# Attention stage: the exchange of halves per head instead of per block, and the word operations of a w_val half spread one to a step

## The chip, the cores and the metric

One core of one Trainium2 chip runs the whole program in one launch. The metric is device time in microseconds (us), the median of repeated executions; before the change three executions took 618.32, 618.34 and 618.87 us. The profile is one further execution, taken by the hardware profiler.

## The reference

The program is a chain of three blocks on a batch of 2 with 8 heads, 768 positions and a head width of 64. Only the first and the start of the second matter here.

```python
q_bits = (einsum(q, proj) > 0); k_bits = (einsum(k, proj) > 0)     # 6 bits: 64 buckets
mask   = q_bucket[:, :, :, None] == k_bucket[:, :, None, :]
scores = where(mask, scale * q @ k.T, -1e9)
attn   = softmax(scores)                                           # exp, sum, divide
x      = attn @ v                                                  # heads side by side: [2, 768, 512]
...
gate = sigmoid(causal_conv(x, conv_w)); val = x @ w_val
x    = (gate * val) @ w_out                                        # second block
...                                                                # third block: FFT mixing, norm, two-layer MLP
```

Matrix weights arrive as float64 words. The kernel turns each into a pair of float32 numbers (high and low part) by integer operations on the words, and multiplies with three matmuls (high by high, high by low, low by high).

## The kernel before

**Pairs and steps.** `attention` goes over eight pairs of heads (p = 0 to 7), each in twelve steps (i = 0 to 11, n = 12p + i; steps are counted from 0 here, as in the code, so the change's "steps 7 to 9" are i = 6, 7, 8). Step i covers 128 query rows of one head; six steps are a head. The order on each engine is written out by hand: whatever a step calls is issued in that order to the engine's queue, and each engine takes its queue strictly in order.

**One step.** PE (TensorE) transposes the probabilities of step n (`ptp`, L593), multiplies the scores of step n + 3 (`sp`, L557, one PSUM buffer), and multiplies with v (`op`, L616, half of a 256-row block per step). DVE (VectorE) clamps the scores of n + 3 out of PSUM (`sd`, L568), then takes the low part of the transposed probabilities (`ptl`, L605). ACT (ScalarE) takes their high part (`pth`, L601), then the exponential of step n + 2 (`sd`, L575), and in odd steps copies a finished block of the product out of PSUM (`xc`, L629). In steps 9 to 11 and 1 to 3 two transposes of the next pair's q and k go beside (L693), with a high part on ACT (`ht`, L698) and a low part on DVE (`lt`, L701). In steps 4 and 5 the bucket bits are projected (`bp`, L443). `qk_place` (L411 to L416, steps 3 and 9) sends those parts by DMA from SP's queue into the tiles that the scores read. `norm_spread` (L644) and `norm_beside` (L666) turn the softmax sums of the pair before into a row that is spread by DMA; `norm_mul` (L719) applies it on POOL (GpSimd).

**The exchange of halves.** A block's product has its high-part sum in 64 partitions and its low-part sum in the other 64. `pv_out` copies the block to `xc`, sends 64 partitions of it by DMA to `xs` (one buffer; L633, on SP's queue), and a step later POOL adds the two into `xm` (L634).

**The words of w_val.** `half_weights` converts a 128 by 256 half of w_val, one half per pair (`val_weights`), with six integer operations on DVE and two on ACT. The words lie in one PSUM tile `cvp`, whose left half is `a` and whose right half is `g`. In order: *magnitude* (L271, DVE, writes a), *rest* (L272, DVE, writes g), *rest_low* (L275, DVE, writes g), *rebias* (L278, ACT, reads and writes a), *sign* (L279, DVE, writes a), *exponent* (L280, DVE, reads a, writes another tile), *low* (L283, DVE, writes `wvl`), *high* (L286, ACT, reads a, writes `wvh`). They are called in five groups, at the end of steps 6 to 10 (7 to 11 in pair 0, 0 to 4 in pair 7).

Of the kernel before, what the change touches and what calls it, by code (L numbers as in the profile page):

```python
# [17 lines left out]
P = 128  # L18
# [86 lines left out]
def block_kernel(  # L105
# [156 lines left out]
    def words_split(raw, dst_h, dst_l, b, a, g):  # L262

        n = raw.shape[1]
        words = raw.bitcast(I32).rearrange("p (n two) -> p n two", two=2)
        lo, hi = words[:, :, 0], words[:, :, 1]
        a, g = a.bitcast(I32), g.bitcast(I32)
        e = ap4.tile([P, DM], I32, tag="cve", name="cv")[:, :n]

        def step0():  # L270
            nc.vector.tensor_scalar(a, hi, 0x7FFFFE00, None, op0=ALU.bitwise_and)  # L271
            nc.vector.tensor_scalar(g, hi, 0x1FF, 15, op0=ALU.bitwise_and, op1=ALU.logical_shift_left)  # L272

        def step1():
            nc.vector.scalar_tensor_tensor(g, lo, 17, g, op0=ALU.logical_shift_right, op1=ALU.bitwise_or)  # L275

        def step2():
            nc.scalar.activation(a, a, AF.Relu, scale=8.0, bias=col[:, b : b + 1])  # L278
            nc.vector.scalar_tensor_tensor(a, hi, -(2 ** 31), a, op0=ALU.bitwise_and, op1=ALU.bitwise_or)  # L279
            nc.vector.tensor_scalar(e, a, -(2 ** 23), None, op0=ALU.bitwise_and)  # L280

        def step3():
            nc.vector.scalar_tensor_tensor(dst_l, g, 2.0 ** -35, e.bitcast(F32), op0=ALU.mult, op1=ALU.mult)  # L283

        def step4():
# [16 lines left out]
    def attention(es):  # L302
# [315 lines left out]
                        start=r == 0 and x == 0, stop=r == R - 1 and x == 1,  # L618
                    )

        def pv_out(kb):
            p, j, blk = kb // 6, (kb % 6) // 3, kb % 3
            if kb % 6 == 0:
                st[p]["xm"] = ap2.tile([P, S], F32, tag="xm", name="xm")
            mr = slice(64 * j, 64 * j + 64)
            cr = slice(64 - 64 * j, 128 - 64 * j)
            xc = ap2.tile([P, QB], F32, tag="xc", name="xc")
            xs = ap2.tile([P, QB], F32, tag="xs", name="xs", bufs=1)
            nc.scalar.copy(xc, po[kb])  # L629
            if kb == 6 * NPR - 1:  # L630
                nc.scalar.copy(xs[mr, :], po[kb][cr, :])
            else:
                nc.sync.dma_start(xs[mr, :], xc[cr, :])  # L633
            add[kb] = lambda: nc.gpsimd.tensor_tensor(  # L634
                st[p]["xm"][mr, blk * QB : (blk + 1) * QB], xc[mr, :], xs[mr, :], op=ALU.add
            )

        def norm_sums(p):
            sums = st[p]["sums"]
# [2 lines left out]
        def norm_spread(p):  # L642
            rinv = st[p]["rinv"] = ap2.tile([P, 2, R], F32, tag="rinv", name="rinv")
            nc.vector.reciprocal(rinv, st[p]["sums"].rearrange("p (j r) -> p j r", j=2))  # L644
            if p < NPR - 1:
                return
            rb = st[p]["rb"] = ap1.tile([P, R, 2, D], F32, tag="rb", name="rb")
# [124 lines left out]
        def val_load(i):  # L772
            c, h = divmod(i, 2)
            wv_raw[i] = ap4.tile([P, DM // 2], I64, tag="wvr", name="wvr", bufs=2)
            nc.sync.dma_start(wv_raw[i], w_val[c * P : (c + 1) * P, h * DM // 2 : (h + 1) * DM // 2])

        def val_weights(i):
            c, h = divmod(i, 2)
            cs = slice(h * DM // 2, (h + 1) * DM // 2)
            return half_weights(wv_raw[i], wvh[:, c, cs], wvl[:, c, cs], 3)  # L780

        def out_tile(i):
            t = qk_tile((0, 2, 1)[i]).rearrange("p a s -> p (a s)")
# [16 lines left out]
        convs = [(b, c, i) for b, c in pairs[: NPR - 1] for i in range(9)]  # L800
        start()
        NT = 12 * NPR
        for n in range(NT + 2):
# [25 lines left out]
            if n + 2 < NT:  # L829
                expo(n + 2)  # L830
            if 0 <= kb < 6 * NPR and part == 1:
                pv_out(kb)
            if n == 6:
                prep_step(1, i)
            if kb - 1 in add and part == 0:
                add.pop(kb - 1)()
            elif n == NT + 1:
                add.pop(kb)()
# [42 lines left out]
            if p < NPR and at <= i < at + 5:
                if i == at:
                    wsteps = val_weights(p)
                    if p + 1 < NPR:
                        val_load(p + 1)
                wsteps[i - at]()
# [123 lines left out]
    def mixing(es):  # L1010
# [419 lines left out]
```

## Time and profile before

| | |
|---|---|
| median of three executions | 618.34 us |
| the profiled execution's own time | 618.59 us |
| its span, first to last instruction | 616.8 us |
| PE busy | 604.7 us (98%) |
| DVE busy | 444.7 us (72%) |
| ACT busy | 358.5 us (58%) |
| POOL busy | 269.3 us (44%) |
| granted TensorE clock | 0.999 of full speed |

The attention stage lies between about 10 and 250 us of the span. A line of a timeline has the start in us from the span's start, the duration, the engine, the line of the kernel, the operation, output and inputs with their shape, and in brackets how long the engine had been idle before it and what ended that. Instructions of an engine overlap a little: the next one starts about 0.08 us before the one ahead has ended on DVE and about 0.10 us on ACT, so that what one costs its engine is the distance to the next start. In a list of windows each line gives a stretch, its length, and for each engine the busy time with the number of instructions.

### The profile page before, as it was taken

The numbers are of one execution on the slowest core, as the hardware profiler recorded it, in microseconds if no ns is written. First come the engines' busy times: TensorE is split into PE (matmuls) and PEld (weight loads), VectorE is DVE, ScalarE is ACT, GpSimd is POOL, SyncE is SP. The second block draws the span as 40 slices with busy tenths as digits, with TensorE's granted clock in tenths as the row PEclk, the third lists the DMA queues.
The fourth block names the chain that finished last, engine by engine and source line by source line (L and its number), as shares of the span: only waits on it lengthen the run. The fifth ranks groups of instructions, "written<-read, shape, count | busy, mean of one in ns | idle before, by whom it ended". The sixth has DMA issues, their size and how long they took to land.

```text
span 616.8 us, 10435 instructions
## 1 busy us (share of the span) xinstructions
PE 604.7 (98%) x3711; PEld 537.4 (87%) x3711; DVE 444.7 (72%) x850; ACT 358.5 (58%) x712; POOL 269.3 (44%) x303
## 2 busy tenths in 40 slices
PE   7999999999999999999999999999999999999997
PEld 6889999999998889998898988888888888888886
DVE  5999999999999998898669788888885411111113
ACT  5998899998998887944625355555665111111121
POOL 8152588876888799892350633233221000000000
PEclk9999999999999999999999999999999999999999
DMA  6956686756666640262110243443440200000002
GB/s 139 210 142 164 145 178 160 164 152 156 157 154 178 171 124 14 73 231 70 36 35 0 70 133 118 125 136 108 134 135 1 103 0 1 2 0 1 0 1 102
DMA packets 54957, 62.02 MB, mean 101 GB/s; under 512 B 29184, under 2 KB 42664, under 8 KB 54650
## 3 DMA queue, kind: packets, MB, share of 16 engines
q1 hardware_dynamic: 54170, 57.81, 35.7%
q0 software_dynamic: 432, 3.55, 1.5%
q8 instruction: 29, 0.48, 0.3%
q14 instruction: 22, 0.18, 0.1%
q10 hardware_dynamic: 304, 0.01, 0.0%
HBM read 36.73 MB, written 3.19 MB: 65 GB/s over the span
## 4 chain that ended last, share of the span: by engine, by line
PE 78%; DVE 10%; DMA 4%; ACT 2%; issue 2%; SPq 2%; POOL 1%; DVEq 0%; ACTq 0%; POOLq 0%
PE pf L1337 20%; PE acc L1347 20%; PE sp L557 8%; PE op L616 7%; PE ptp L593 6%; PE ps L1154 5%; PE ps L222 3%; PE ps L1218 3%; DVE sd L568 2%; DVE ptl L605 2%; PE ps L1189 1%; DMA rqk<-in_k_dram 1%; PE late L222 1%; DMA xs<-xc 1%; PE bp L443 1%
## 5 line engine op out<-in xcount | busy, mean ns | idle before, releaser
L1347 PE MATMUL acc<-w,hid 128*128 128x512 f32 x576 | 137.4, 391 | 0.0
L1347 PEld LDWEIGHTS acc<-w,hid 128*128 128x128 f32 x576 | 105.5, 188 | 20.1
L1340 DVE SCALAR_TENSOR_TENSOR hid<-pf,hid 128x512 fp32r<-128x512 f32 (+1 forms) x62 | 33.4, 555 | 120.6 <-ACT hid L1339 120.6
L1337 PE MATMUL pf<-uth,w 128*128 128x512 f32 (+1 forms) x496 | 97.1, 337 | 0.1
L568 DVE TENSOR_SCALAR_CACHE_REDUCE sd<-sp 128x768 f32<-128x768 f32 x96 | 91.1, 950 | 7.7 <-PE sp L557 7.2
L1339 ACT ACTIVATE hid<-pf 128x512 fp32r<-128x512 f32 (+1 forms) x62 | 28.9, 488 | 115.2 <-PE pf L1337 115.2
L557 PE MATMUL sp<-qk 128*128 128x512 f32 (+1 forms) x384 | 91.5, 360 | 3.9 <-DVE sd L568 2.6
L605 DVE TENSOR_TENSOR ptl<-ptp,pth 128x768 fp32r<-128x768 f32 x96 | 91.4, 952 | 5.1 <-ACT pth L601 3.8
L1337 PEld LDWEIGHTS pf<-uth,w 128*128 128x128 f32 x496 | 79.0, 188 | 15.2 <-DVE hid L1340 1.3
L575 ACT ACTIVATE sd<-sd,nm 128x768 f32<-128x768 f32 x96 | 90.1, 939 | 1.5 <-DVE sd L568 1.5
L601 ACT CAST pth<-ptp 128x768 fp32r<-128x768 f32 x96 | 77.0, 802 | 17.7 <-PE ptp L693 8.9
L162 POOL TENSOR_TENSOR w<-cv 128x512 fp32r<-128x512 f32 x31 | 40.1, 1293 | 88.8 <-DVE cv L157 77.4
L593 PE MATMUL ptp<-ident,sd 128*128 128x128 f32 x576 | 78.6, 272 | 0.2 <-ACT sd L575 0.2
L616 PE MATMUL op<-pth,v 128*128 128x256 f32 x288 | 74.0, 283 | 1.0 <-ACT xc L629 1.0
L616 PE MATMUL op<-ptl,v 128*128 128x256 f32 x288 | 73.8, 286 | 0.0
L557 PEld LDWEIGHTS sp<-qk 128*128 128x128 f32 x384 | 58.2, 189 | 13.6 <-DVE sd L568 7.1
L593 PEld LDWEIGHTS ptp<-ident,sd 128*128 128x128 f32 x576 | 65.8, 140 | 1.1 <-ACT sd L575 0.5
L634 POOL TENSOR_TENSOR xm<-xc,xs 64x256 f32<-64x256 f32 x48 | 35.2, 734 | 59.2 <-DMA xs<-xc 38.6
L616 PEld LDWEIGHTS op<-pth,v 128*128 128x128 f32 x288 | 54.2, 188 | 5.9 <-ACT xc L629 2.0
L616 PEld LDWEIGHTS op<-ptl,v 128*128 128x128 f32 x288 | 54.3, 188 | 0.3
L1337 PE MATMUL pf<-utl,w 128*128 128x512 f32 (+1 forms) x248 | 53.1, 336 | 0.0
L149 ACT ACTIVATE cv<-cv,col 128x512 int32<-128x512 int32 x32 | 23.2, 725 | 41.5 <-DVE cv L146 41.5
(214 smaller groups left out, 998.0 us busy)
## 6 DMA issues: line engine op xcount, KB each, us to landing
raw<-in_moe_w_ch_dram SPq DMA_DIRECT2D x32, 512.0 KB
qk<-ht SPq DMA_DIRECT2D x60, 192.0 KB
qk<-lt SPq DMA_DIRECT2D x30, 192.0 KB
rqk<-in_q_dram SPq DMA_DIRECT2D x16, 192.0 KB
rqk<-in_k_dram SPq DMA_DIRECT2D x16, 192.0 KB
rv<-in_v_dram SPq DMA_DIRECT2D x8, 384.0 KB
out_dram<-o SPq DMA_DIRECT2D x12, 256.0 KB
xs<-xc SPq DMA_DIRECT2D x47, 64.0 KB
```

The lines of the kernel that those rows point to most:

```text
L162: nc.gpsimd.tensor_tensor(dst()[1], fold(g.bitcast(F32)), fold(e.bitcast(F32)), op=ALU.mult)
L557: nc.tensor.matmul(sp[:, cs], q2[i][:, m, qi * P : (qi + 1) * P], k2[i][:, m, cs], start=m == order[0], stop=m == order[1])
L568: nc.vector.tensor_scalar(sd[n], sp, CLAMP, None, op0=ALU.min, op1=ALU.min, accum_out=st[p]["nm"][:, n % 12 : n % 12 + 1],)
L575: nc.scalar.activation(sd[n], sd[n], AF.Exp, bias=st[p]["nm"][:, i : i + 1], scale=-1.0, accum_out=st[p]["sums"][:, i : i + 1],)
L593: nc.tensor.transpose(tp[:, r // 3, c0 : c0 + P], sd[n][:, r * P : (r + 1) * P], ident)
L601: nc.scalar.copy(p_parts(n)[0], tp)
L605: nc.vector.tensor_tensor(lo, tp, f32(ho), op=ALU.subtract)
L616: nc.tensor.matmul(po[kb], v3[:, r, c0 : c0 + P], pt[kb][x][:, r, :], start=r == 0 and x == 0, stop=r == R - 1 and x == 1,)
L634: add[kb] = lambda: nc.gpsimd.tensor_tensor(st[p]["xm"][mr, blk * QB : (blk + 1) * QB], xc[mr, :], xs[mr, :], op=ALU.add)
L1337: nc.tensor.matmul(pf, w[:, c, :], x[:, c, cs], start=n == 0, stop=n == 3 * NC - 1)
L1340: nc.vector.scalar_tensor_tensor(hl[:, cs], pf, 0.0, f32(hh)[:, cs], op0=ALU.max, op1=ALU.subtract)
L1347: nc.tensor.matmul(acc, x[:, ts_], w, start=f == 0 and n == 0, stop=f == NF - 1 and n == 2)
```

## The change

Three edits, all in `attention` and its helper for the words.

1. `pv_out`: `xc` holds a whole head (three blocks) and `xs` is gone. The DMA goes straight into the half of `xm` that the head will own, once per head after its third block (192 KB in place of three times 64 KB), and POOL adds `xc` to `xm` once per head, two steps after the DMA is issued. The last head keeps its exchange per block, because its blocks are wanted one by one.
2. The eight word operations become functions of their own. In pairs 1 to 5 they are called in six groups at steps 6, 7, 8 and at steps 0, 1, 2 of the next pair, with one DVE operation each. Pairs 0, 6 and 7, and the words of w_out, keep their five groups.
3. In pair 7 the row of sums is transposed in step 3 rather than 1, its spreading DMA is issued in step 4 rather than 2, and the product follows in step 6 rather than 5; `rb` takes the buffer of `rv`.

```diff
+WV = (0, 1, 2, 6, 7, 8)
...
+        return magnitude, rest, rest_low, rebias, sign, exponent, low, high
+
+    def in_five(steps):
+        groups = (0, 1), (2,), (3, 4, 5), (6,), (7,)
+        return [lambda x=x: run(steps[i] for i in x) for x in groups]
...
-        def pv_out(kb):
+        def pv_out(n, kb):
...
-            xc = ap2.tile([P, QB], F32, tag="xc", name="xc")
-            xs = ap2.tile([P, QB], F32, tag="xs", name="xs", bufs=1)
-            nc.scalar.copy(xc, po[kb])
+            cs = slice(blk * QB, (blk + 1) * QB)
+            nc.scalar.copy(xc[:, cs], po[kb])
             if kb == 6 * NPR - 1:
-                nc.scalar.copy(xs[mr, :], po[kb][cr, :])
+                nc.scalar.copy(xm[mr, cs], po[kb][cr, :])
+                at = n
+            elif kb >= 6 * NPR - 3:
+                nc.sync.dma_start(xm[mr, cs], xc[cr, cs])
+                at = n + 1
+            elif blk < 2:
+                return
             else:
-                nc.sync.dma_start(xs[mr, :], xc[cr, :])
+                cs = slice(0, S)
+                nc.sync.dma_start(xm[mr, :], xc[cr, :])
+                at = n + 2
+            add[at] = lambda: nc.gpsimd.tensor_tensor(xm[mr, cs], xc[mr, cs], xm[mr, cs], op=ALU.add)
...
-            if 1 <= p and i == (1 if p == NPR - 1 else 4):
+            if 1 <= p and i == (3 if p == NPR - 1 else 4):
                 return norm_beside(p - 1)
...
+            if not 1 <= i < NPR - 2:
+                return dict(enumerate(in_five(steps)))
+            return dict(zip(WV, [lambda x=x: run(steps[i] for i in x) for x in ((0,), (1,), (2, 3), (4,), (5, 7), (6,))]))
```

Where the instructions stand now is shown at three places. **First**, DVE in steps 7 to 9 of pair 1, before:

```order
L605 TENSOR_TENSOR ptl<-ptp,pth 128x6x128
L275 SCALAR_TENSOR_TENSOR cvp<-wvr,cvp 128x256
L568 TENSOR_SCALAR sd,nm<-sp 128x768
L605 TENSOR_TENSOR ptl<-ptp,pth 128x6x128
L279 SCALAR_TENSOR_TENSOR cvp<-wvr,cvp 128x256
L280 TENSOR_SCALAR cv<-cvp 128x256
L568 TENSOR_SCALAR sd,nm<-sp 128x768
L605 TENSOR_TENSOR ptl<-ptp,pth 128x6x128
L701 SCALAR_TENSOR_TENSOR lt<-ptp,col,ht 128x256
L283 SCALAR_TENSOR_TENSOR wvl<-cvp,cv 128x256
```

and now (L616 is `ptl`, L579 the clamp, L720 `lt`; L275 is now *rest* and L278 *rest_low*):

```order
L616 TENSOR_TENSOR ptl<-ptp,pth 128x6x128
L275 TENSOR_SCALAR cvp<-wvr 128x256
L579 TENSOR_SCALAR sd,nm<-sp 128x768
L616 TENSOR_TENSOR ptl<-ptp,pth 128x6x128
L278 SCALAR_TENSOR_TENSOR cvp<-wvr,cvp 128x256
L579 TENSOR_SCALAR sd,nm<-sp 128x768
L616 TENSOR_TENSOR ptl<-ptp,pth 128x6x128
L720 SCALAR_TENSOR_TENSOR lt<-ptp,col,ht 128x256
```

*rest_low* has moved from step 7 to step 8, behind that step's `ptl`; *sign*, *exponent* and *low* have left these steps. *rebias* keeps its place on ACT, behind the exponential of step 8 and ahead of the high parts of step 9:

```order
L586 ACTIVATE sd,sums<-sd,nm 128x768 [waits DVE_49]
L281 ACTIVATE cvp<-cvp,col 128x256 [waits DVE_49,Activation_49]
L612 CAST pth<-ptp 128x6x128 [waits PE_49]
L717 ACTIVATE ht<-ptp,col 128x256 [waits DMAHW5_49,DMAHW6_49,DMAHW4_49,DMAHW3_49]
L586 ACTIVATE sd,sums<-sd,nm 128x768
L642 COPY xc<-op 128x256 [waits PE_49,Pool_49]
```

**Second**, ACT and DVE in steps 1 and 2 of pair 2. ACT from the exponential of step 1 on, before and now:

```order
L575 ACTIVATE sd,sums<-sd,nm 128x768 [waits DVE_49,Activation_49]
L629 COPY xc<-op 128x256 [waits DMAHW6_49,PE_49,Pool_49]
L601 CAST pth<-ptp 128x6x128 [waits PE_49,Activation_49]
L698 ACTIVATE ht<-ptp,col 128x256
L575 ACTIVATE sd,sums<-sd,nm 128x768 [waits DVE_49]
```

```order
L586 ACTIVATE sd,sums<-sd,nm 128x768 [waits DVE_49,Activation_49]
L642 COPY xc<-op 128x256 [waits PE_49]
L293 CAST wvh<-cvp 128x256 [waits DVE_49]
L612 CAST pth<-ptp 128x6x128 [waits PE_49,Activation_49]
L717 ACTIVATE ht<-ptp,col 128x256
L586 ACTIVATE sd,sums<-sd,nm 128x768
```

DVE there now (L287 is *exponent*, L290 *low*, L663 the reciprocal of `norm_spread`):

```order
L616 TENSOR_TENSOR ptl<-ptp,pth 128x6x128
L720 SCALAR_TENSOR_TENSOR lt<-ptp,col,ht 128x256
L287 TENSOR_SCALAR cv<-cvp 128x256
L579 TENSOR_SCALAR sd,nm<-sp 128x768
L616 TENSOR_TENSOR ptl<-ptp,pth 128x6x128
L720 SCALAR_TENSOR_TENSOR lt<-ptp,col,ht 128x256
L663 RECIPROCAL rinv<-sums 128x12
L290 SCALAR_TENSOR_TENSOR wvl<-cvp,cv 128x256
```

*high* (L293) has come from step 10 of the pair before to step 1, between the block's copy and the high part of step 2; *exponent* and *low* stand behind the `lt` of steps 1 and 2.

**Third**, SP's queue from step 7 to step 9 of pair 1, before and now (`wvr` is the next half of w_val, `rs` the spread row):

```order
L775 DMA wvr<-in_moe_w_val_dram 128x256
L633 DMA xs<-xc 64x256
L680 DMA rs<-rd 64x768 x2
L633 DMA xs<-xc 64x256
L411 DMA qk<-ht 64x768
L412 DMA qk<-ht 64x768
```

```order
L794 DMA wvr<-in_moe_w_val_dram 128x256
L653 DMA xm<-xc 64x768
L699 DMA rs<-rd 64x768 x2
L422 DMA qk<-ht 64x768
L423 DMA qk<-ht 64x768
```

The exchange of step 9 that stood ahead of `qk_place` is gone, and with it the wait for `xs`, the one buffer that POOL's add gives back.

## Rows read from the trace of the kernel before

**Rows 1.** Page, part 4: the chain that ended last, by engine.

```profile
PE 78%; DVE 10%; DMA 4%; ACT 2%; issue 2%; SPq 2%; POOL 1%; DVEq 0%; ACTq 0%; POOLq 0%
```

**Rows 2.** Windows from step 6 of pairs 2, 4, 5 to the next pair's.

```profile
89.40:117.90 28.50, 28.22 (x215) 26.72 (x214) 27.27 (x52) 25.85 (x54) 23.94 (x27) 1.00 0.72 168
...
146.39:175.57 29.18, 28.67 (x215) 26.68 (x214) 27.22 (x51) 26.58 (x57) 24.57 (x28) 1.00 0.65 154
175.57:205.04 29.47, 28.63 (x215) 26.78 (x214) 27.24 (x52) 26.53 (x55) 26.62 (x32) 1.00 0.64 161
```

**Rows 3.** Timeline of PE, steps 7 and 8 of pair 2.

```profile
89.91 0.82 PE L593 MATMUL ptp<-ident,sd 128*128 128x128 f32 x6
90.48 0.94 PE L557 MATMUL sp<-qk 128*128 128x512 f32 x4
...
91.97 0.82 PE L593 MATMUL ptp<-ident,sd 128*128 128x128 f32 x6
93.07 0.96 PE L557 MATMUL sp<-qk 128*128 128x512 f32 x4 [0.28 <-DVE sd L568]
```

**Rows 4.** Timeline of DVE, steps 7 and 9 of pair 2.

```profile
92.93 0.95 DVE L605 TENSOR_TENSOR ptl<-ptp,pth 128x768 fp32r<-128x768 f32 x1
93.80 0.42 DVE L275 SCALAR_TENSOR_TENSOR cvp<-wvr,cvp 128x256 int32<-128x256 int32 x1
...
98.41 0.47 DVE L701 SCALAR_TENSOR_TENSOR lt<-ptp,col,ht 128x256 fp32r<-128x256 f32 x1
```

**Rows 5.** Timeline of ACT, steps 8 and 9 of pair 2.

```profile
94.50 0.44 ACT L278 ACTIVATE cvp<-cvp,col 128x256 int32<-128x256 int32 x1
95.71 0.80 ACT L601 CAST pth<-ptp 128x768 fp32r<-128x768 f32 x1 [0.77 <-PE ptp L693]
96.40 0.48 ACT L698 ACTIVATE ht<-ptp,col 128x256 fp32r<-128x256 f32 x1
96.77 0.94 ACT L575 ACTIVATE sd<-sd,nm 128x768 f32<-128x768 f32 x1
...
97.69 0.37 ACT L629 COPY xc<-op 128x256 f32<-128x256 f32 x1
```

**Rows 6.** Timeline of ACT, then DVE: later conversions of w_out.

```profile
243.03 0.45 ACT L278 ACTIVATE cvp<-cvp,col 128x256 int32<-128x256 int32 x1 [0.41 <-DVE cvp L275]
...
259.98 0.59 ACT L286 CAST qk<-cvp 128x512 fp32r<-128x512 f32 x1 [0.65 <-DVE cv L280]
...
258.53 0.69 DVE L279 SCALAR_TENSOR_TENSOR cvp<-wor,cvp 128x512 int32<-128x512 int32 x1
```

**Rows 7.** Timeline: ACT and DVE in step 1 of pair 5, ACT in step 1 of pair 6.

```profile
163.38 0.47 ACT L698 ACTIVATE ht<-ptp,col 128x256 fp32r<-128x256 f32 x1 [0.67 <-DMA qk<-ht]
163.88 0.96 DVE L605 TENSOR_TENSOR ptl<-ptp,pth 128x768 fp32r<-128x768 f32 x1 [0.31 <-ACT ht L698]
...
192.89 0.47 ACT L698 ACTIVATE ht<-ptp,col 128x256 fp32r<-128x256 f32 x1 [1.00 <-DMA qk<-ht]
```

**Rows 8.** Waits of SP's queue: total us, times, longest.

```profile
SPq L633 <- POOL xm L634: 25.7, 21, 2.9
```

**Rows 9.** Timeline, DVE and PE, first steps of pair 7.

```profile
218.50 0.96 DVE L568 TENSOR_SCALAR_CACHE_REDUCE sd<-sp 128x768 f32<-128x768 f32 x1 [0.23 <-PE sp L557]
...
220.53 0.28 PE L666 MATMUL ptp<-ident,rinv 128*12 128x128 f32 x1 [0.68 <-DVE rinv L644]
...
221.54 0.96 DVE L568 TENSOR_SCALAR_CACHE_REDUCE sd<-sp 128x768 f32<-128x768 f32 x1 [0.28 <-PE sp L557]
```

**Rows 10.** Timeline, DVE, ACT and PE, steps 1 to 4 of pair 3.

```profile
106.50 0.95 DVE L605 TENSOR_TENSOR ptl<-ptp,pth 128x768 fp32r<-128x768 f32 x1
...
107.26 0.80 ACT L601 CAST pth<-ptp 128x768 fp32r<-128x768 f32 x1
...
108.79 0.95 DVE L605 TENSOR_TENSOR ptl<-ptp,pth 128x768 fp32r<-128x768 f32 x1
...
111.39 0.95 PE L557 MATMUL sp<-qk 128*128 128x512 f32 x4
```

More of the change, by code (lines that the diff above doesn't have):

```diff
@@ L268, in words_split, with magnitude, rest, rest_low @@
         e = ap4.tile([P, DM], I32, tag="cve", name="cv")[:, :n]
-        def step0():
+        def magnitude():
             nc.vector.tensor_scalar(a, hi, 0x7FFFFE00, None, op0=ALU.bitwise_and)
+        def rest():
             nc.vector.tensor_scalar(g, hi, 0x1FF, 15, op0=ALU.bitwise_and, op1=ALU.logical_shift_left)
-        def step1():
+        def rest_low():
             nc.vector.scalar_tensor_tensor(g, lo, 17, g, op0=ALU.logical_shift_right, op1=ALU.bitwise_or)
-        def step2():
+        def rebias():
             nc.scalar.activation(a, a, AF.Relu, scale=8.0, bias=col[:, b : b + 1])
+        def sign():
             nc.vector.scalar_tensor_tensor(a, hi, -(2 ** 31), a, op0=ALU.bitwise_and, op1=ALU.bitwise_or)
+        def exponent():
             nc.vector.tensor_scalar(e, a, -(2 ** 23), None, op0=ALU.bitwise_and)
-        def step3():
+        def low():
             nc.vector.scalar_tensor_tensor(dst_l, g, 2.0 ** -35, e.bitcast(F32), op0=ALU.mult, op1=ALU.mult)
-        def step4():
+        def high():
             nc.scalar.copy(dst_h, a.bitcast(F32))
-        return [step0, step1, step2, step3, step4]
+        return magnitude, rest, rest_low, rebias, sign, exponent, low, high
+    def in_five(steps):
+        groups = (0, 1), (2,), (3, 4, 5), (6,), (7,)
+        return [lambda x=x: run(steps[i] for i in x) for x in groups]
     def half_weights(raw, dst_h, dst_l, b):
@@ L624, in pv_out @@
                 st[p]["xm"] = ap2.tile([P, S], F32, tag="xm", name="xm")
+            if blk == 0:
+                st[p]["xc"] = ap2.tile([P, S], F32, tag="xc", name="xc")
+            xm, xc = st[p]["xm"], st[p]["xc"]
             mr = slice(64 * j, 64 * j + 64)
             cr = slice(64 - 64 * j, 128 - 64 * j)
-            xc = ap2.tile([P, QB], F32, tag="xc", name="xc")
-            xs = ap2.tile([P, QB], F32, tag="xs", name="xs", bufs=1)
-            nc.scalar.copy(xc, po[kb])
+            cs = slice(blk * QB, (blk + 1) * QB)
+            nc.scalar.copy(xc[:, cs], po[kb])
             if kb == 6 * NPR - 1:
-                nc.scalar.copy(xs[mr, :], po[kb][cr, :])
-            else:
-                nc.sync.dma_start(xs[mr, :], xc[cr, :])
-            add[kb] = lambda: nc.gpsimd.tensor_tensor(
-                st[p]["xm"][mr, blk * QB : (blk + 1) * QB], xc[mr, :], xs[mr, :], op=ALU.add
-            )
+                nc.scalar.copy(xm[mr, cs], po[kb][cr, :])
[5 more added lines that the diff above has]
+                return
+            else:
+                cs = slice(0, S)
+                nc.sync.dma_start(xm[mr, :], xc[cr, :])
+                at = n + 2
+            add[at] = lambda: nc.gpsimd.tensor_tensor(xm[mr, cs], xc[mr, cs], xm[mr, cs], op=ALU.add)
         def norm_sums(p):
@@ L646, in norm_spread @@
                 return
-            rb = st[p]["rb"] = ap1.tile([P, R, 2, D], F32, tag="rb", name="rb")
+            rb = st[p]["rb"] = ap1.tile([P, R, 2, D], F32, tag="rv", name="rb")
             pool_copy(
@@ L779, in val_weights @@
             cs = slice(h * DM // 2, (h + 1) * DM // 2)
-            return half_weights(wv_raw[i], wvh[:, c, cs], wvl[:, c, cs], 3)
+            steps = half_weights(wv_raw[i], wvh[:, c, cs], wvl[:, c, cs], 3)
+            if not 1 <= i < NPR - 2:
+                return dict(enumerate(in_five(steps)))
+            return dict(zip(WV, [lambda x=x: run(steps[i] for i in x) for x in ((0,), (1,), (2, 3), (4,), (5, 7), (6,))]))
         def out_tile(i):
@@ L790, in out_half @@
             cs = slice(i * DM // 2, (i + 1) * DM // 2)
-            return half_weights(wo_raw[0][:, cs], wo_h[0][:, cs], wo_l[0][:, cs], 4)
+            return in_five(half_weights(wo_raw[0][:, cs], wo_h[0][:, cs], wo_l[0][:, cs], 4))
         tail = []
@@ L798, in val_early @@
             val_matmul(0, 0, c, tail[c])
+        wsteps = {}
         convs = [(b, c, i) for b, c in pairs[: NPR - 1] for i in range(9)]
@@ L831, in attention @@
             if 0 <= kb < 6 * NPR and part == 1:
[L832 to L838, printed above, removed]
+                pv_out(n, kb)
+            if n in add:
+                add.pop(n)()
             if n == 0:
                 values(0, 1)
-            if p + 1 < NPR and n != 6:
+            if p + 1 < NPR:
                 prep_step(p + 1, i)
@@ L851, in attention @@
             last = p == NPR - 1
-            if i == (2 if last else 7) and 1 <= p < NPR:
+            if i == (4 if last else 7) and 1 <= p < NPR:
                 norm_rows(p - 1)
-            if i == (5 if last else 10) and 1 <= p < NPR:
+            if i == (6 if last else 10) and 1 <= p < NPR:
                 norm_mul(p - 1)
@@ L880, in attention @@
             at = 0 if last else 7 if p == 0 else 6
[L881 to L886, printed above, removed]
+            if p < NPR and i == at:
+                wsteps = {n + x: f for x, f in val_weights(p).items()}
+                if p + 1 < NPR:
+                    val_load(p + 1)
+            if n in wsteps:
+                wsteps.pop(n)()
             for _ in range(1 if n >= NT - 16 else 5 * n // 6 - 5 * (n - 1) // 6):
@@ L1066, in chunk @@
             a, g_ = (x.tile([P, DM], F32, tag=y, name="cvp") for x, y in ((psm, "m"), (pso, "o")))
-            return words_split(wo_raw[c], wo_h[c], wo_l[c], 4, a, g_)
+            return in_five(words_split(wo_raw[c], wo_h[c], wo_l[c], 4, a, g_))
         def gated(c):
```

## Prediction

> **What bounds the kernel now.** I read the page first. The chain that ended last is PE for 78% and DVE for 10% [rows 1], so time is lost where PE waits for something, and a change beside PE pays only as far as such a wait moves. Then the windows from pair to pair: a pair of the attention stage takes 28.50 us (pairs 1 to 3 agree within 0.01), and ACT, DVE and PE are all nearly full in it, 25.85, 27.27 and 28.22 busy; two later pairs took 29.18 and 29.47 [rows 2]. The timelines show what a step is made of. PE's bare step is 2.06 us from `ptp` to `ptp`, and in step 8 the scores start at 93.07 though the transposes were through at 92.54 (0.57 after their start, as in step 7): PE waited 0.53 for the clamp [rows 3]. The clamp was late because DVE had two word operations in step 6. A word operation holds DVE 0.34, a `ptl` or clamp 0.87, an `lt` 0.39, each its duration less the overlap of 0.08 [rows 4].
>
> A Trainium skill page, Perfetto Trace Analysis, section Identifying the Most-Contended Engine, calls busy share a fair measure of headroom for the vector and scalar engines. By that ACT has 28.50 - 25.85 = 2.65 us per pair to spare, and the two waits below would vanish in it.
>
> **What the change adds: two waits of ACT for DVE.** That is the term that decides. *rebias* (ACT) changes one half of the tile `cvp`, and *rest_low* (DVE) writes the other half ahead of it in the program. The waits go by the tile: in a later conversion *rebias* was idle 0.41 until *rest_low* (L275) ended, though *magnitude* had ended long before; and *high* (L286) was idle 0.65 until *exponent* (L280), although *sign* (L279), the last to write what it reads, had ended 0.76 earlier, at 259.22 [rows 6]. Before, this cost nothing in pairs 1 to 5: *rest_low* ran in step 7 and *rebias* in step 8, *exponent* in step 8 and *high* in step 10. Now *rest_low* and *rebias* are called in one step, and so are *exponent* and *high*, and ACT's queue holds the high parts of the next step behind them.
>
> *Wait at step 8.* Let its clamp start at t. DVE then does the clamp and `ptl` (0.87 each) and *rest_low* (0.42): ended at t + 2.16. With 0.06 for the signal, *rebias* starts at t + 2.22, where before it started when ACT was free (94.50). Behind it stand, with ACT's distances from start to start [rows 5], *rebias* itself (0.36), `pth` of step 9 (0.69), `ht` (0.37), the exponential (0.92) and the copy `xc` (0.37 long): t + 2.22 + 0.36 + 0.69 + 0.37 + 0.92 + 0.37 = t + 4.93. `op` of step 10 needs the PSUM buffer that this copy empties, and PE gets there at t + 4.31: its scores of step 8 start 1.07 before t, a step with transposes beside is 2.29 (`ptl` to `ptl` [rows 10]), and `op` stands 0.80 behind its scores: -1.07 + 2 x 2.29 + 0.80 = 4.31. With 0.06 for the signal again, PE waits 4.99 - 4.31 = 0.68.
>
> *Wait at step 1.* `ptl` starts at T (106.50 in pair 3 [rows 10]). DVE does it, `lt`, and now *exponent*: T + 0.87 + 0.39 + 0.42 = T + 1.68. *high* starts at T + 1.74 and takes 0.29, so `pth` of step 2 starts at T + 2.03, 108.53 in place of 107.26 [rows 10]. `ptl` waits for the end of `ht`, not of `pth` alone, as it did at 163.88 [rows 7]: 0.69 + 0.48 + 0.06 later, at 109.76 in place of 108.79, 0.97 late. *low* adds 0.34 on DVE ahead of the clamp of step 3. DVE's slack on this stretch is small (0 to 0.25; I take 0.18), so the scores of step 4 come 0.97 + 0.34 - 0.18 = 1.13 later than 111.39.
>
> Both prices are bounded by what the chip charged for a late ACT in step 1: ACT idle for 0.67 and 1.00 [rows 7], and the pairs longer by 29.18 - 28.50 = 0.68 and 29.47 - 28.50 = 0.97 [rows 2]. So a late ACT is paid in full there, even in pairs with ACT busy for 26.58 of 29.18. The trace thus speaks against the rule above, and I give it a small chance only. The lower bound of the two waits is nothing; the upper is all that ACT starts late, 1.41 (t = 93.69, so *rebias* at 95.91) plus 1.27 = 2.68.
>
> **What the change takes away.** *Two word operations in a row in step 6.* The clamp of step 7 starts 0.45 earlier (0.34, and 0.11 between two operations on one tile), and of PE's 0.53 I count 0.45. In steps 7 to 11 DVE has 11.35 us of work (five clamps and `ptl`, three `lt`, four word operations with 0.12 between two of them) against PE's 2 x 2.06 + 3 x 2.29 = 10.99, so up to 0.36 more was lost there; I take 0.25. Together 0.70 per pair.
>
> *The exchange per block.* SP's queue is in order, and its issue of `xs` waited for POOL's add 21 times, 25.7 us in all [rows 8], because `xs` has one buffer. Behind the one in step 9 stand the six DMAs of `qk_place`, which must have read `ht` before ACT may overwrite it in step 1 of the next pair. That is the 0.67 and 1.00 in pairs 5 and 6, where POOL was fullest (24.57 and 26.62). Now no exchange stands ahead of them, and the one of step 7 waits for ACT's copy alone: the two stalls go, 0.68 + 0.97 = 1.65. What it adds: one 192 KB transfer in place of three of 64 KB, the same bytes; and a 64 by 768 add where three of 64 by 256 were, less POOL time. In pairs 1 to 3 the old waits of POOL and SP held up nothing, so nothing is gained there. Next late would be POOL's add, if a whole head takes more than two steps (4.3 us) to land; nothing on PE waits for it soon, so I cost it at zero, bounded by 0.3 per pair.
>
> *Pair 7.* PE waited 0.68 for the reciprocal in step 1 [rows 9], and the clamps were 221.54 - 218.50 = 3.04 apart. With the transpose in step 3, DVE sets the distance: clamp 0.88, `ptl` 0.87, reciprocal 0.14, two word operations 0.45 and 0.34, 2.68. Gain 0.36. The row arrives some two steps later and is wanted one step later; POOL has that time.
>
> Moved at no cost: the fewer DMA issues on SP, `rb` in the buffer of `rv`, the ACT copies (the same count), and the word operation *sign* in step 0, where DVE has 1.74 of work and PE 2.06.
>
> **The sum.** Per pair 0.68 + 1.13 - 0.70 = +1.11; five pairs +5.55. Then -1.65 - 0.36: +3.54. On the profiled execution's 618.59 that is 622.1, and since the median of the runs lies 0.25 below it, **621.9**.
>
> **The rivals.**
> *A. The spread works and the waits are hidden.* For it: ACT's idle share, the rule above. Against: rows 7 with rows 2. Mechanism: ACT catches up before `ptl` and `xc` are wanted. Then a pair gains 0.70 and loses only what *exponent*, the reciprocal and *low* push DVE past PE in steps 1 and 2, about 0.25: 5 x -0.45 - 2.01 = -4.3, 614.1. It decides from an ACT slack of over 0.7 at step 8 and 1.1 at step 2. By the skill's rule the result is this one.
> *B. One of the two waits is hidden,* the one at step 8, since ACT was idle 0.77 ahead of `pth` of step 9 [rows 5]. I have counted that idle time already, but the copy may be earlier than I make it. Per pair 1.13 - 0.70 = +0.43; 2.15 - 2.01 = +0.1: 618.5, no change.
> *C. Slower still.* The waits are paid in full, as rows 7 suggest, or POOL's add comes late too: per pair up to 2.68 - 0.70 = 1.98, +7.9 in all, 626.2; half way to it 624.
>
> **How the numbers follow.** About 0.2% (1.24 us) is what a measurement of this kernel can tell from no change: the bounds are 617.1 and 619.6. My forecast has 0.67 (620 to 623.5), A 0.12, B 0.13, C 0.08. Faster: A and a little of B, 0.13. Same: most of B and the low edge of the forecast, 0.14. Slower: 0.73. The likeliest case's own range is 620.0 to 623.5; the range that holds 8 in 10 takes in B and the lower half of C: 617.2 to 624.2. It leaves out A and the top of C.
>
> **What would show it.** Right: in pairs 2 to 5 a pair takes about 29.5; ACT's list of waits has a new entry, *rebias* and *high* waiting for DVE word operations, some 1.3 and 1.0 us each, five times; PE waits for `xc` in step 10; DVE waits for `ht` in step 2; step 6 shortens from 2.66 to about 2.2; no ACT wait for the DMA of `qk`. Wrong: pairs at or under 28.2 with those waits there (then A), or the stall for `qk` still in pairs 5 and 6, or POOL waiting long for `xm`.

## The result, and the profile after

The changed kernel took a median of 624.81 us over four executions (624.57 to 624.91) against 618.33 for the kernel before (617.86 to 618.87): a ratio of 1.0099, with a 95% interval of 1.008 to 1.0118. It is slower, as forecast, but by 6.5 us where 3.5 were predicted, and 0.6 above the top of the range. The profiled execution took 624.85; its span is 623.1. One of the executions of the kernel before that were run beside the experiments below took 848.92 us at a granted clock of 0.656; the ratios leave it out, the median of 618.35 there has it in.

The windows from step 6 of one pair to step 6 of the next, of the kernel after (pairs 0, 2, 4, 5 and 6; columns as in [rows 2]):

```profile
31.58:61.58 30.00, 29.16 (x215) 26.95 (x215) 28.53 (x56) 26.18 (x55) 9.94 (x13) 1.00 0.64 146
...
91.18:120.78 29.60, 28.56 (x215) 26.62 (x214) 27.33 (x52) 25.70 (x54) 22.75 (x22) 1.00 0.71 160
...
150.37:180.38 30.01, 28.55 (x215) 26.61 (x214) 27.33 (x51) 26.71 (x57) 23.55 (x24) 1.00 0.69 158
180.38:209.98 29.60, 28.55 (x215) 26.62 (x214) 27.33 (x51) 26.30 (x55) 23.91 (x25) 1.00 0.62 151
209.98:237.40 27.42, 26.71 (x199) 24.66 (x198) 26.52 (x52) 24.09 (x49) 24.70 (x22) 1.00 0.49 119
```

A pair now takes 29.60, where it took 28.50. The last three windows answer to 29.18, 29.47 [rows 2] and 27.78 before. ACT's work is the same (25.70 busy, 25.85 before); what has grown is the time in which it waits. Its list of waits between 60 and 210 us, with the waits behind it (total, times, longest):

```profile
DVE ptl L616 <- ACT ht L717: 6.5, 10, 1.1
ACT cvp L281 <- DVE cvp L278: 6.4, 5, 1.3
ACT wvh L293 <- DVE cv L287: 4.7, 5, 0.9
...
PE op L627 <- ACT xc L642: 2.4, 5, 0.5
```

Both waits named in the prediction are there, five times each: *rebias* (L281) for *rest_low* (L278), *high* (L293) for *exponent* (L287). No wait of ACT for the DMA of `qk` is left. The chain of waits that ended last has moved with them, from PE 78% and DVE 10% [rows 1] to

```profile
PE 73%; DVE 15%; ACT 5%; issue 3%; DMA 2%; SPq 0%; POOL 0%; ACTq 0%; DVEq 0%; POOLq 0%
```

**Step 8, in the timelines** of DVE, ACT and PE, pair 2. The clamp of step 8 starts at t = 95.45:

```profile
95.45 0.95 DVE L579 TENSOR_SCALAR_CACHE_REDUCE sd<-sp 128x768 f32<-128x768 f32 x1
...
97.19 0.42 DVE L278 SCALAR_TENSOR_TENSOR cvp<-wvr,cvp 128x256 int32<-128x256 int32 x1
...
97.71 0.45 ACT L281 ACTIVATE cvp<-cvp,col 128x256 int32<-128x256 int32 x1 [1.32 <-DVE cvp L278]
...
100.05 0.38 ACT L642 COPY xc<-op 128x256 f32<-128x256 f32 x1
...
99.05 0.95 PE L568 MATMUL sp<-qk 128*128 128x512 f32 x4
...
100.48 0.39 PE L627 MATMUL op<-pth,v 128*128 128x256 f32 x1 [0.48 <-ACT xc L642]
```

*rest_low* ends at t + 2.16, *rebias* starts at t + 2.26 and the copy ends at t + 4.98; t + 2.16, 2.22 and 4.93 were forecast. By the prediction's 0.80 behind the scores of 99.05, `op` could have started at 99.85: PE lost 0.63 (the trace, in which the matmul ahead still runs out, shows it idle for 0.48).

**Steps 1 and 2**, pair 3 (DVE, ACT, PE), where the `ptl` of step 1 starts at T = 108.31:

```profile
108.31 0.95 DVE L616 TENSOR_TENSOR ptl<-ptp,pth 128x768 fp32r<-128x768 f32 x1
...
109.57 0.41 DVE L287 TENSOR_SCALAR cv<-cvp 128x256 int32<-128x256 int32 x1
...
110.02 0.37 ACT L293 CAST wvh<-cvp 128x256 fp32r<-128x256 f32 x1 [0.94 <-DVE cv L287]
110.29 0.81 ACT L612 CAST pth<-ptp 128x768 fp32r<-128x768 f32 x1
...
111.50 0.96 DVE L616 TENSOR_TENSOR ptl<-ptp,pth 128x768 fp32r<-128x768 f32 x1 [0.64 <-ACT ht L717]
112.38 0.47 DVE L720 SCALAR_TENSOR_TENSOR lt<-ptp,col,ht 128x256 fp32r<-128x256 f32 x1
...
113.00 0.85 PE L604 MATMUL ptp<-ident,sd 128*128 128x128 f32 x6 [0.32 <-DVE rinv L663]
...
114.19 0.97 PE L568 MATMUL sp<-qk 128*128 128x512 f32 x4 [0.23 <-DVE sd L579]
```

`ptl` of step 2 starts at T + 3.19 (before T + 2.29 [rows 10]), the scores of step 4 at T + 5.88 (before 111.39 - 106.50 = 4.89): 0.99 later, with 1.13 forecast. A part of it goes a way that the prediction did not have: PE's transposes of step 4 (113.00) also start late, since by the program they wait for the `lt` of step 2 (112.38), which reads the `ptp` buffer that they need; the reciprocal that the row names is DVE's next operation, and PE needs it only for a later transpose.

**Where the 6.26 us between the two profiled executions are** (starts of the same work, before and after; the last row by SP's last issue):

| stretch | before | after | difference | forecast |
|---|---|---|---|---|
| start to the first clamp | 11.40 | 11.85 | +0.45 | 0 |
| first clamp to step 6 of pair 1 | 49.51 | 49.73 | +0.22 | 0 |
| pairs 1 to 3, step 6 to step 6 | 85.48 | 88.79 | +3.31 | +3.33 |
| pair 4 to pair 5 | 29.18 | 30.01 | +0.83 | +0.43 |
| pair 5 to pair 6 | 29.47 | 29.60 | +0.13 | +0.14 |
| pair 6 to step 6 of pair 7 | 27.78 | 27.42 | -0.36 | -0.36 |
| step 6 of pair 7 to the last accumulation | 371.87 | 372.14 | +0.27 | 0 |
| from there to the end | 12.1 | 13.5 | +1.4 | 0 |

The attention pairs came out at +3.91 where +3.54 was forecast. The rest, some 2.3 us, lies where the prediction had looked at nothing: in the first microseconds, in pair 0, in the third block and after the last matmul.

### The profile page after: what moved, and what is told of

The parts are those of the page before. It is cut to its first block, busy times and chain, and to the rows that moved or that the text cites. A ratio compares the mean times of both kernels' runs of the same rounds, so it can differ in the third digit from the quotient of the medians.

```text
span 623.1 us, 10290 instructions
## 1 busy us (share of the span) xinstructions
PE 606.5 (97%) x3711; PEld 537.7 (86%) x3711; DVE 444.5 (71%) x850; ACT 358.1 (57%) x712; POOL 264.7 (42%) x273
## 3 DMA queue, kind: packets, MB, share of 16 engines
HBM read 36.73 MB, written 3.19 MB: 64 GB/s over the span
## 4 chain that ended last, share of the span: by engine, by line
PE 73%; DVE 15%; ACT 5%; issue 3%; DMA 2%; SPq 0%; POOL 0%; ACTq 0%; DVEq 0%; POOLq 0%
PE pf L1356 20%; PE acc L1366 19%; PE sp L568 6%; PE op L627 5%; PE ps L1173 5%; DVE ptl L616 4%; PE ptp L604 4%; DVE sd L579 4%; PE ps L223 3%; PE ps L1237 3%; DMA rs<-rd 1%; PE ps L1208 1%; PE bp L454 1%; PE late L223 1%; ACT sd L586 1%
## 5 line engine op out<-in xcount | busy, mean ns | idle before, releaser
L616 DVE TENSOR_TENSOR ptl<-ptp,pth 128x768 fp32r<-128x768 f32 x96 | 91.6, 954 | 10.8 <-ACT ht L717 6.5
L579 DVE TENSOR_SCALAR_CACHE_REDUCE sd<-sp 128x768 f32<-128x768 f32 x96 | 91.3, 951 | 7.3 <-PE sp L568 6.1
L242 POOL TENSOR_TENSOR g<-g,conv_tmp 128x768 f32<-128x768 f32 x27 | 46.7, 1728 | 1.6
```

What stands on the lines that cost most here:

```text
L242: nc.gpsimd.tensor_tensor(dst, dst, tmp, op=ALU.add)
L579: nc.vector.tensor_scalar(sd[n], sp, CLAMP, None, op0=ALU.min, op1=ALU.min, accum_out=st[p]["nm"][:, n % 12 : n % 12 + 1],)
L616: nc.vector.tensor_tensor(lo, tp, f32(ho), op=ALU.subtract)
```

## The experiments

The theory: two waits by the tile, on ACT, cost 0.7 and 0.7 to 1.1 per pair; the late end has a cause of its own. The rivals: ACT makes the waits good and the time is DVE's; the end is noise, or belongs to one of two queues that the change made shorter. The kernel before, run beside them, had medians of 618.35, 619.0 and 618.48 in the three groups of runs and otherwise scattered from 616.8 to 621.5.

### Each wait alone, and both

**rebias_later**:

```diff
-WV = (0, 1, 2, 6, 7, 8)
+WV = (0, 1, 2, 3, 6, 7, 8)
-... ((0,), (1,), (2, 3), (4,), (5, 7), (6,))
+... ((0,), (1,), (2,), (3,), (4,), (5, 7), (6,))
```

> Only rebias is moved, one step later (step 9), so that ACT no longer meets rest_low of the same step. If the wait of rebias is what costs pairs 2 to 6 their time around step 8 (+0.72 each by the two clamp intervals after it, 2.80 + 2.52 against 2.47 + 2.13), the time is 624.8 - 5 x 0.72 = 621.2 and these two intervals are back at about 2.47 and 2.13. If ACT had made that wait good and the added time is DVE's own work, it stays at 624.8.

Measured: 621.01 us, ratio 1.0056 (1.0039 to 1.0073). Between pairs 2 and 3:

```profile
89.82:118.66 28.84, 28.28 (x215) 26.61 (x214) 27.25 (x52) 25.66 (x54) 22.89 (x22) 1.00 0.70 163
```

28.84 in place of 29.60: this wait costs 0.76 a pair.

**high_first**:

```diff
-... (4,), (5, 7), (6,)
+... (4,), (7, 5), (6,)
```

> Only the order within one group is changed: high is called ahead of exponent, so ACT waits for sign of the step before and no longer for exponent. If that wait is the cost of steps 1 and 2 (+1.14 per pair in pairs 2 to 6, +0.41 more in pair 5 where a cast of x stands behind high), all of it goes but about 0.25 per pair of DVE's own work: 624.8 - 5 x 0.9 - 0.4 = 619.9. If DVE's exponent, low and reciprocal are the cost, the time stays within 1 us of 624.8.

Measured: 620.54 us, ratio 1.0043 (1.0029 to 1.0058), between the two theories' numbers and near the first. The same window:

```profile
90.49:119.37 28.88, 28.36 (x215) 26.60 (x214) 27.24 (x51) 25.72 (x54) 22.83 (x22) 1.00 0.71 165
```

The wait is 0.72 a pair, not 0.9. What remains of steps 1 and 2 is DVE's: the clamps of steps 1 to 4 there stand 2.48 + 2.54 + 2.14 apart (2.29 + 2.29 + 2.17 before), 0.41 more for *exponent*, *low* and the reciprocal.

**no_waits** has both edits.

> Both at once: rebias one step later and high ahead of exponent. If the two waits add up, 624.8 - 3.6 - 4.9 = 616.3, faster than both kernels, with a pair at 27.9 to 28.1. If one only hides behind the other, the gain is the larger of the two alone and the time about 620.

Measured: 616.19 us, ratio 0.9965 (0.9949 to 0.9981), faster than both kernels.

```profile
89.61:117.72 28.11, 28.09 (x215) 26.61 (x214) 27.16 (x52) 25.64 (x54) 22.85 (x22) 1.00 0.75 168
```

28.11 a pair, 1.49 under the changed kernel: 0.76 and 0.72 add up. Against 28.50 the spread, less the DVE work that it puts into steps 1 and 2, is worth 0.39.

### The halves of the change

**exchange_only**: every pair keeps the five groups.

```diff
-            if not 1 <= i < NPR - 2:
-                return dict(enumerate(in_five(steps)))
-            return dict(zip(WV, [...]))
+            return dict(enumerate(in_five(steps)))
```

> The exchange per head and pair 7's edit, with the words in their five groups as before. If the exchange takes away the stalls of ht in pairs 5 and 6, they come back to 28.5 (-0.68 and -0.97) and pair 7 gains 0.36: -2.0, against +0.23 seen in pair 0. Then 616.6 with an end like that of before. Two theories of the late end part here. If it goes by SP's queue (385 instructions, as short as the changed kernel's 390), the end costs 1.0 to 1.4 more: 617.8. If it goes by the moment of DVE's last fetch of instructions (DVE has 878, as the kernel with the longer SP queue had), the end is within 0.4 of before: 616.8. If the stalls had another cause, 618.3 or more.

Measured: 617.69 us, ratio 0.9979 (0.9964 to 0.9995). Its windows of pairs 0, 4, 5 and 6:

```profile
31.18:61.19 30.01, 29.17 (x215) 26.95 (x215) 28.53 (x56) 26.19 (x55) 9.96 (x13) 1.00 0.66 147
...
146.70:175.20 28.50, 28.21 (x215) 26.70 (x214) 27.28 (x51) 26.58 (x57) 23.55 (x24) 1.00 0.73 169
175.20:203.70 28.50, 28.21 (x215) 26.66 (x214) 27.28 (x52) 26.46 (x55) 23.99 (x25) 1.00 0.68 161
203.70:231.10 27.40, 26.67 (x199) 24.62 (x198) 26.51 (x51) 24.09 (x49) 24.92 (x23) 1.00 0.49 119
```

The stalls of pairs 5 and 6 are gone to the hundredth, and pair 7 gains 0.38. The median is 0.9 above the 616.8 expected, the profiled execution (617.45) 0.6: of that 0.2 lie in the third block, which is longer with this half alone too, and 0.3 in a longer end. Pair 0 took 0.27 more, near the 0.23 that I had put in.

**words_only**: the kernel before with the six groups, the exchange per block kept (the edit is against the kernel before).

```diff
+WV = (0, 1, 2, 6, 7, 8)
...
+            return dict(zip(WV, [lambda x=x: run(steps[i] for i in x) for x in ((0,), (1,), (2, 3), (4,), (5, 7), (6,))]))
...
+                wsteps = {n + x: f for x, f in val_weights(p).items()}
```

> The six groups of the words alone, with the exchange per block and pair 7 as before. If waits and stalls add up: pair 1 to 2 -0.71, four times +1.11, once +1.82 and 0.41 for the cast of x in pair 5, +6.0 in all: 624.3. If the qk stalls of pairs 5 and 6 hide under the new waits, 622.7. The end, by SP's queue (459 instructions): as before. By DVE's last fetch (873 instructions, about 4 us ahead of the last data, as in the two kernels with high first): 0.9 more, 625.2.

Measured: 624.70 us, ratio 1.0089 (1.0058 to 1.012). Of the stalls for `qk` one is left, in pair 6, on top of the new waits:

```profile
197.03 0.47 ACT L709 ACTIVATE ht<-ptp,col 128x256 fp32r<-128x256 f32 x1 [0.50 <-DMA qk<-ht]
...
199.78 0.37 ACT L293 CAST wvh<-cvp 128x256 fp32r<-128x256 f32 x1 [1.10 <-DVE cv L287]
```

In pair 5 none is left (30.02 from step 6 to step 6, against 30.01 in the changed kernel), presumably because a slower pair gives POOL and SP more time; no run shows that alone. From the first clamp to step 6 of pair 7, words_only is 5.35 longer than the kernel before and exchange_only 1.76 shorter, together +3.59, where the whole change has +4.13. So the two halves nearly add up, and the whole loss there is the words'.

### The late end

Behind the last issue of output (614.24 before, 619.08 after) the span goes on for 2.6 us before and 4.0 after. The DMA view of the kernel after from 612.72 to its end shows one fetch of instructions just as the last output lands (busy tenths in 40 slices; queue, packets, MB, share):

```profile
DMA  0000000000000799999999999999920000000000
...
q14 instruction: 1, 0.01, 0.2%
```

**longer_queue**:

```diff
-            nc.sync.dma_start(r, w_ch2[fs, :])
+            for x in (slice(0, DM // 2), slice(DM // 2, DM)):
+                nc.sync.dma_start(r[:, x], w_ch2[fs, x])
...
+            for c in (slice(0, NC // 2), slice(NC // 2, NC)):
...
```

> The changed kernel, with each load of an MLP weight (third block, SP's queue) issued in two halves: 32 more issues on SP, the same bytes and all the rest the same. The changed kernel's span goes on 2.6 us after the last output data where before it was 1.4, and one fetch of instructions stands there. If that fetch is of SP's own queue, whose length it changed (454 to 390 instructions), a queue of 426 has it elsewhere: 623.4. If it is another engine's (POOL went from 440 to 387), or the late end has nothing to do with the fetch, 624.8.

Measured: 623.35 us, ratio 1.009 (1.0066 to 1.0114), as the first theory said, yet it does not show it: the split also gave DVE's queue ten more wait instructions (878 for 868), and in the four kernels of this group the fetch had moved with DVE's count, not with SP's. So the theory that it is SP's was put against another, that it is DVE's, by

**dve_pad**:

```diff
+        pad = ap1.tile([P, 1], F32, name="pad")
+        for _ in range(16):
+            nc.vector.memset(pad, 0.0)
```

> The changed kernel with 16 writes of one column (0.06 us each) on DVE while it is idle at the start; SP's queue is not touched. If the late end goes by where DVE's last fetch of instructions falls, it moves well ahead of the output and the end is as before: 624.8 - 1.4 = 623.4. If it goes by SP's queue, 624.8.

Measured: 622.89 us, ratio 1.0066 (1.0046 to 1.0086). SP's queue is that of the changed kernel, and its end is 2.9 us, with no fetch in the last 10 us. That is 1.1 of the 1.9 by which its median is shorter; in its profile most of the rest lies ahead of the first clamp (11.12, where the changed kernel has 11.85; see the start, below).

```profile
DMA  0000000000000000069999999999998993000000
```

The words' half alone, whose SP queue is longer than that of before, has the fetch in the middle of the output, a dip in the transfers with it, and 3.3 us of end:

```profile
DMA  0000000000000007999899959999999920000000
...
q14 instruction: 1, 0.01, 0.4%
```

| kernel | DVE's queue, instructions | fetch within the output | last issue to the end |
|---|---|---|---|
| before | 883 | none | 2.6 |
| own_tile (below) | 865 | none; 1 us behind the end | 2.9 |
| the change, rebias_later, cast_later (below) | 868 | at its last packets | 4.0, 4.0, 4.0 |
| words_only, high_first, no_waits | 873 | about 4 us ahead of them | 3.3, 3.6, 3.5 |
| exchange_only, longer_queue | 878 | none | 2.9, 2.9 |
| dve_pad, no_waits_pad | 884, 889 | none | 2.9, 2.9 |

The counts are those of the built programs; each trace has 94 more records of DVE. The fetch comes later as DVE's count falls, and dve_pad changed that count alone. So the fetch of DVE's next instructions, moved into the last output by 15 instructions fewer (10 by the words, 5 by the exchange), costs 0.6 to 1.1 us.

Another 0.3 of the end is SP's. The full traces, which have every instruction by itself, show its last ones: six waits, 0.06 us apart, always for the same semaphores in the same order. In the kernel before and in words_only the last output signals a semaphore of the sixth wait, and the span goes on for 1.25 and 1.28 us behind its last packet. In all the others it signals one of the first; five waits follow, 5 x 0.06 = 0.3, and the span goes on for 1.53 to 1.57 where no fetch falls among the last packets (2.1 where one does). The 1.4 and 2.6 in the expectation of longer_queue are coarser readings of the same stretch.

**no_waits_pad**, the best version:

> The version with neither wait, and the same 16 writes on DVE at the start. By DVE's last fetch the end loses the 0.9 that it has over before: 615.3. By SP's queue it stays at 616.2.

Measured: 615.43 us, ratio 0.9945 (0.9923 to 0.9967), with an end of 2.9 in place of 3.5.

### The tile, and the cast in pair 5

**own_tile**:

```diff
...
-        e = ap4.tile([P, DM], I32, tag="cve", name="cv")[:, :n]
...
+        cv = ap4.tile([P, DM], I32, tag="cve", name="cv")
+        e = cv[:, :n]
+        g = cv[:, n : 2 * n] if g is None else g.bitcast(I32)
...
```

> The changed kernel, every instruction in its place, but the half g (rest, rest_low, low) lies in the free half of the SBUF tile cv, so that rebias and rest_low touch different tiles; exponent and high still share a. If the wait of rebias for rest_low goes by the tile and not by the numbers, it vanishes without any step being moved: the clamp intervals after step 8 fall from 2.80 + 2.52 to 2.29 + 2.29 as in the kernel with rebias later, and the time is 624.8 - 3.7 = 621.1. If it was rebias's place in ACT's queue, or DVE's work there, 624.8. The wait of high stays (3.28 in step 2) by either.

Measured: 631.41 us (627.24 to 633.21), ratio 1.0192 (1.0148 to 1.0235): a miss by time. The wait itself is gone with nothing moved; all that *rebias* waits for now is this, once:

```profile
ACT cvp L283 <- DVE cvp L274: 0.6, 1, 0.6
```

But *rest_low* and *low* now take both inputs from SBUF, and beside POOL's operations they take some three times as long (DVE, then POOL, of this kernel):

```profile
97.20 1.42 DVE L280 SCALAR_TENSOR_TENSOR cv<-wvr,cv 128x256 int32<-128x256 int32 x1
...
112.73 1.18 DVE L292 SCALAR_TENSOR_TENSOR wvl<-cv 128x256 fp32r<-128x256 int32 x1
...
96.48 1.86 POOL L242 TENSOR_TENSOR g<-g,conv_tmp 128x768 f32<-128x768 f32 x1
...
111.79 1.83 POOL L657 TENSOR_TENSOR xm<-xc,xm 64x768 f32<-64x768 f32 x1 [2.36 <-DMA xm<-xc]
```

That POOL does it shows within the run: where POOL has nothing running as they start, the same two operations take 0.41 and 0.36. One of these places is pair 1, and there the run shows the price of the wait as well:

```profile
67.29 0.41 DVE L280 SCALAR_TENSOR_TENSOR cv<-wvr,cv 128x256 int32<-128x256 int32 x1
...
143.23 0.36 DVE L292 SCALAR_TENSOR_TENSOR wvl<-cv 128x256 fp32r<-128x256 int32 x1
...
66.43 0.44 ACT L283 ACTIVATE cvp<-cvp,col 128x256 int32<-128x256 int32 x1
```

*rebias* starts ahead of *rest_low* of its own step, and the next clamps stand 2.29 + 2.29 apart, as with rebias_later, where the changed kernel has 2.80 + 2.52; from step 7 to step 11 pair 1 is 0.76 shorter. Thus the run shows that the wait goes by the tile, and in pair 1 its price. The kernel before shows the same with both halves in PSUM: in three of its later conversions of w_out each half has a PSUM tile of its own, and in all three *rebias* starts before *rest_low* has ended, here while it runs:

```profile
256.10 0.70 DVE L275 SCALAR_TENSOR_TENSOR cvp<-wor,cvp 128x512 int32<-128x512 int32 x1
...
256.44 0.65 ACT L278 ACTIVATE cvp<-cvp,col 128x512 int32<-128x512 int32 x1
```

A version of the changed kernel with g in a PSUM tile of its own was not tried.

**cast_later**:

```diff
-            if p == 5 and i in (1, 3, 5, 7):
-                x_split(0, 0, i // 2)
+            if p == 5 and i in (2, 3, 5, 7):
+                x_split(0, 0, (i - 1) // 2)
```

> The changed kernel with the first cast of x in pair 5 called in step 2 and not in step 1, where it stands behind high. If the 0.41 by which pair 5's step 2 is longer than that of the other pairs (3.69 against 3.28) is this cast, started late behind the wait of high, the interval falls to 3.28 and the time to 624.4. If it is POOL's or SP's, it stays 3.69 and 624.8.

Measured: 624.23 us, ratio 1.0089 (1.0063 to 1.0116). In the changed kernel, pair 5 (ACT, then DVE):

```profile
169.22 0.37 ACT L293 CAST wvh<-cvp 128x256 fp32r<-128x256 f32 x1 [0.95 <-DVE cv L287]
...
169.49 0.52 ACT L201 CAST xh<-xT 128x384 fp32r<-128x384 f32 x1
169.90 0.80 ACT L612 CAST pth<-ptp 128x768 fp32r<-128x768 f32 x1
...
171.11 0.96 DVE L616 TENSOR_TENSOR ptl<-ptp,pth 128x768 fp32r<-128x768 f32 x1 [1.05 <-ACT ht L717]
```

With the cast a step later `ptl` follows 0.64 late, as in the other pairs, and the interval is 3.27 in place of 3.69. Step 4 is 0.18 longer for it, so that the pair gains 0.27 (29.74 for 30.01):

```profile
170.35 0.96 DVE L616 TENSOR_TENSOR ptl<-ptp,pth 128x768 fp32r<-128x768 f32 x1 [0.64 <-ACT ht L717]
```

## Why the prediction was right, and where not

**Right: the mechanism, its places and the sum per pair.** Pairs 1 to 3 gave +3.31 where +3.33 stood; the copy `xc` and the two waits came at the forecast moments. That the sum fits to 0.02 is in part luck: by the experiments the first term below was 0.08 too small and the second about as much too large.

- *Wait at step 8*: 0.68 forecast, 0.76 by taking it away.
- *Wait at step 1*: 1.13 forecast with what *low* and DVE add; 0.72 for the wait and 0.3 to 0.4 for DVE, by taking it away. Rival A's 0.25 for that DVE part was too low.
- *Two word operations in a row in step 6*: step 6 fell from 2.66 to 2.20, and the one stretch that has the spread without a wait, from step 9 of pair 0 to step 9 of pair 1, is 0.71 shorter (0.70 forecast).
- *The exchange per block*: the stalls of 0.68 and 0.97 went. *Pair 7*: -0.36 as forecast.
- *Rival A* would have had the two waits vanish in ACT's idle share of 2.65 us per pair. It took as room for waits what the Trainium skill (Perfetto Trace Analysis, Identifying the Most-Contended Engine) calls a fair measure of how close such an engine is to its limit. The waits cost 1.49, at ACT busy for 25.70 of 29.60. Where the prediction weighed the rule against [rows 7], the rows were right: idle time after the waiting instruction's deadline does not help.

**Wrong: the size of the sum, +3.54 for +6.26.** The step that failed is the sum: it added the pairs alone, all five at a price read from pairs 2 and 3, and put everything else at zero ("moved at no cost"). The runs showed these terms in its place, of which the end alone is more than the 0.6 by which the time lies above the range:

- *Pair 5, +0.40.* The wait of *high* was priced from pair 3's queue. In pair 5 a cast of x stands behind *high* as well, and `pth` starts later by it. cast_later shows it.
- *Pair 0, +0.2.* With the exchange of step 6 gone, POOL adds a part of v at a moment when DVE has an operation with both inputs in SBUF. Before, and then now, DVE and then POOL:

```profile
35.34 0.27 DVE L761 TENSOR_TENSOR cwr<-cwr 20x128 f32<-20x128 f32 x1
```

```profile
35.76 0.70 DVE L780 TENSOR_TENSOR cwr<-cwr 20x128 f32<-20x128 f32 x1
...
35.31 1.01 POOL L400 TENSOR_TENSOR v<-rv,v 128x384 fp32r<-128x384 f32 x1
```

  exchange_only has it too (0.71). In words_only, where POOL's addition of the old exchange starts just ahead of it, it takes 0.55; before, that addition started 0.08 behind it (35.42). Each time that it is held it ends 0.14 to 0.15 behind POOL's operation. So it goes by which of the two starts first, and most of the +0.2 comes with the exchange half (+0.24 in exchange_only, +0.05 in words_only). That DVE is held by POOL is read from these rows and own_tile's, not from a run of its own.
- *The end, +1.4*, the largest. The prediction counted SP's issues for their time, and no engine's instructions for where the next ones are loaded. dve_pad and the table show 1.1 of it; the other 0.3 is SP's five waits behind the last output, and comes with the exchange half (exchange_only has it, words_only has not).
- *The start, +0.45.* The matmuls that PE does before the data arrive are the same, and ran slower. Before, then after:

```profile
1.72 3.75 PE L356 MATMUL idle<-zeros 128*128 128x256 f32 x18 [1.72 <-POOL zeros L351]
```

```profile
1.72 4.21 PE L367 MATMUL idle<-zeros 128*128 128x256 f32 x18 [1.72 <-POOL zeros L362]
```

  The full traces have each of the eighteen by itself. In the changed kernel they start 0.213 us apart to the end, which is 256 columns at the 1.2 GHz level. Before, they come down to 0.12 us after the fourteenth, at 4.8 us; there, at 4.77, the trace's record of the granted clock begins, at 1.00, while in the changed kernel it begins at 7.03. So the clock rose 2.3 us later behind the same matmuls. rebias_later, whose program is that of the changed kernel up to there, had the rise at 5.07 and its first clamp at 11.16; over the kernels that share this start the rise lay between 4.66 and 7.46 us and the first clamp between 11.16 and 11.85. So this goes with the execution and not with the change.
- *The third block, +0.27*, stays open. It arises between 350 and 450 us; exchange_only has 0.24 of it, words_only 0.08.

Rival C had the right time, 624, by the wrong means: the waits were not dearer than forecast.

## What to carry to other kernels

When an operation is moved to even out one engine, look at which steps of *other* engines share its tile: a producer and a consumer that used to be a step apart and are now called in the same one make a wait, and its price is set by the first thing behind it that someone needs, not by the engine's idle share. Here moving the consumer one step on, or calling the reader ahead of the other reader, turned a loss of 6.5 us into a gain of some 2 (no_waits). Add up the whole program, not the stretch that the change is about: the first and the last microseconds, and the one pair in which something else stands in the queue, made 2.3 of the 6.3.

## What was not expected of the hardware

- A fetch of 8 KB of instructions among the last packets of the output held the end back by 1.1 us (4.0 against 2.9 from the last issue), one about 4 us ahead of them by 0.6 to 0.8; where it falls depends on how many instructions DVE's queue holds. The Trainium skill (Runtime: NRT & Kernel Launch, Instruction fetch mechanics) calls the cost of going from one block of instructions to the next mostly hidden. For a block fetched among the last packets the rows of the end do not agree; what the other fetches cost, no run here shows.
- A DVE operation with both inputs in SBUF took 1.42 and 1.18 us beside a POOL operation of 1.8, where with one input in PSUM it took 0.42 and 0.36. With both inputs in SBUF and no POOL operation running as it started it took 0.41 and 0.36. The Trainium skill (SBUF — State Buffer, SBUF: two separate sides) has the rule that whichever of two such operations starts first holds the port pair that they share for its whole length, and the other is blocked. The rows agree: POOL's started first, and DVE's ended 0.28 and 0.29 us behind it.
- *exponent* and *high* only read what they share, and yet one waited for the other: on this PSUM tile the program keeps two readers on two engines apart as well (0.94 of idle time, five times). Calling *high* first removed 0.72 a pair.
